# Float64 weights into float32 words by ACT and DVE, w_in without identity products, and a new issue order

## The chip, the cores and the metric

One Trainium2 chip, one of its cores. The metric is the device time of one launch in microseconds (us), the median of several runs. PE is the matmul engine, ACT the scalar engine, DVE the vector engine, POOL the general one; SP issues nearly all transfers (DMAs).

## The reference

Inputs: q, k, v of 8 batches x 8 heads x 576 rows x 64, and p of 8 x 8 x 32 x 64, all float32; w_in (512 x 1024), conv_w (3 x 1024) and w_out (1024 x 512) come out of NumPy as float64.

```python
packed = softmax(p @ k.T / 8) @ v                # 32 packed rows a head
attn   = softmax(q @ packed.T / 8) @ packed      # 576 rows a head
x      = attn with the heads side by side        # 8 x 576 x 512
h      = relu(x @ w_in)                          # 8 x 576 x 1024
conv   = sum over t of conv_w[t] * h shifted by t - 1 along the 576 rows
out    = (h * sigmoid(conv)) @ w_out             # 8 x 576 x 512, float32
```

## The kernel before

**Stages.** The 64 heads are taken as 16 groups g of four heads, two groups a batch b. Per group: k and q are loaded and transposed (`load_kq`, `head_transpose`: by PE with an identity for the first four groups, by DVE blocks after that), p is scaled and transposed (`queries`), and `attention(g)` does both softmaxes: PE makes scores, DVE the maxima `nm` and the sums, ACT the exponentials, and DVE leaves the second softmax transposed, as two float32r parts `a2hi` and `a2lo`. Per batch `packed_weight(b, hf)` multiplies the packed rows into w_in (L581), once for each half hf of its 1024 columns, and splits the product into `ghi` and `glo`; `ffn1(b, j)` multiplies that with a2 (L633), one of eight column blocks j at a time, and ACT and DVE do relu, convolution, gate and product into `hgt`. `ffn2(m)` takes 128 rows of the output at a time, 36 tiles m: ACT and DVE split `hgt` into `xhi` (L679) and `xlo` (L682), PE does 24 products with `wo_hi` and `wo_lo` (L698, tiles `fo` and `sm`), ACT copies the result to `o` (L703), SP sends it.

**Weights.** A weight comes as eight pieces i of 128 x 1024 float64, pieces 0 to 3 w_in, 4 to 7 w_out; each half of w_in's columns is two pieces, so `packed_weight(b, 1)` needs piece 3. SP loads a piece (`load_weight`, L296) as pairs of 32-bit words, 1024 KB, into one of three buffers (`stage`, and two in the unused `hgt[1]`). A float64's upper word holds sign, exponent and the first mantissa bits, its lower word the rest. `f64_parts` lets ACT read the upper words as float32 with a Prelu (L267: its scale undoes the exponent's other bias, its alpha does so for negative numbers), DVE shift (L269) and mask (L271) that into the leading part `t`, and DVE multiply the lower words by its power of two (L273) into the rest. Then PE adds the two parts in PSUM: `ident` times `t` and `minus` times the negative rest (L325), and ACT copies the sum out (L329): for w_in to `w_in_sb`; for w_out PE also subtracts `wo_hi`, the leading part rounded to float32r by ACT (L318), and the copy is `wo_lo`. conv_w goes the same way in small, with a DVE addition (L340) in place of PE.

**Order.** Every stage is a generator whose pieces are queued on an engine one at a time, and the table `ORDER` (two characters a piece) says which generator goes on next. An engine works in exactly that order; semaphores hold a piece until what it reads is there. The class `Flow` plays the table with estimated durations while the kernel is built and fills foreseen gaps of PE with `idle` products (L243), until the first `ffn2` tile has been issued; it decides nothing else.

Of the kernel before, what the change touches and what calls it, by code (L numbers as in the profile page):

```python
# [18 lines left out]


ORDER = (
    "3l3k3k3k3k3k3k3m000303033k3k0404040b0802040b3q0g0b0505010j06060c0c0c0j060j060c3u0o0r060e090e07070k053r3r3r3r0k06"
    "0e0k060k050f0e06060e3v0m0f0m0m06060s0s3v0a063v0e0e0m0m0s0r0r3s0d063v060s0606060n060d3r3w3t3t0n3t0d0d0u0e0e0u3r0u"
    "3n0h0i400p0q3t3v3x3v0e3t06063t0l0l0e3x0e3x0e0e0m0m46463y0l0l0w0m0u463x3x0e060e0e0v0e41410v4141460z0m0u0m0m0u420t"
    "3x41410e0u0e0z0m0m3z0e3z0m0m3z480t0z0t0u410m480u0t3z484717473z0m100u0u0m4849494747124a0u480u494912434848434a4944"
    "173z4312120u4a4a0u3z49174a130u494b434c454a4a154b4b4b131f124c434c4d4g1f0m0m4b4b4g4d454c0m434c4d4c4g0u4b0u4c4d434g"
    "4e4e1f4f0u0u4e14454d4d1k0x1c4h4h0u454d4f4e12124h4f4f124i45454e4f4h180y1n4e4e4i4f4f124i1a4i1a451n4j4k6e6e1a1a4i4j"
    "1a4i4j1g1b4i4k4k4j114k164j4k6f4j6f4k1n1b6e6e6e6e6e6e4l6e6e6e4l4j4k1i12121i6g4l1i1a1a1o194l6e1e1d6f6f4m4m1j4m1i1i"
    "4m4l4m126g121a1a4l4l1j6f6f6f4n6f6f4n124m1i1i1q1q1q1a1a6f4m1a126f6h3o6h1v1a4o4o4o4o4p4p4n4n1r1v1q1a6g6g6g6g6g201l"
    "6f6g6g6g1v4p6g4q4r23236h12121a124n4p4p1a4n12124o4o1q1t1s1w4o1r1a4n234p4p6i6h6h6h6h6h6h6h6h4q6h1a126i1y1q1q1y1y1a"  # L30
    "1a4q1m1a6i6i6i6i1i1y6i241h28216g6j4r4r1i1y6j4s4s4s4s1z4s1z4s6i6i6i6k6i1i1y261y4t1i261i4u4s4t4t4u262b1p6k1i4t4t4v"
    "4v6i1u1q6j6j4v1q4v272c4v6j26262b2b4u4t4u6j6j6j6j6j4v4v4u6j6j1q6l50271q1q1x1q502e504u1i1i4w4w4w4u1q1q4w4t1i2e2e4w"
    "3p4w6l1i294w1i6k6k6k2f2f6k6k6k6k6k2g4x6k2k4y2j1i1q4x4y6m4y4x4y6m6l1y1y226l4y6l4z4z2o6k1i4z4z1q4x6l6l6l6l6l4y6l1q"
    "1i4z26511y5126511q4y1q4x4x1q2e6m266m6m6m6m6m1y4x1y264z4z52532j2e6n536m6m251y6n2j525252526m2m2m53525352532e265426"
    "2m6o53532r2n2s6n6n6n6n555a1y6n546n546n6m2e541y5655552654546o545556566n6n2m6p572r2r57261y1y55566l2w552z572a5a2m1y"
    "6p565655566o6o6o6o6o6o2z6o1y1y2n58582z6o6o575a572626262d596p6q6q1y6p2h6o6p6p6p6p6p2e6p57585959585858596p6p2e3726"
    "5b5b2u5826572q59592626592m2e2e266q6q6q6q6q6q6q6r6r6q6s2i5b2u2e6s2p5c5c2u5c5d2m5c5c2e5e5d6q6q2u2m6n5e5e5c2e5d302x"
    "6r6r6r6r6r6r6r2u2m5c5d5d5d5e5e2v5f6r5d5e5f2u5k5g2v2e2e2e5e2e6r6r345f5g5k2u2l5h6s5h5h2e5f5k5f6s5h5h5f5f6s6s37376s"
    "2u32322m2m2e5i6s6s6s3f6t5h6s5i5i3c5h2m2t6t2u2m2m5j5i2m5i6u325g5j6t6t2m2m6u5g2m6t3e386t5i6t6t6t6t3f5j6t6t5g2e2m2u"
    "5l325g5g5j2m2m6v6v325j5j6u6u6u6u6u6u6u5i6u6u5m5l3f366u5m5m332u2u332u5j5m5m6v5n5n5n3a3a325n3g5o6w5m5m3a5o5o5o5l32"  # L40
    "355o5o5n5n5o6v6v6v3b6v3a5n3b5p6v5p2u3a6v32326v5q5p5q5q5r5r6w2y5u5u315q3i6v3a325p5p6v5q3i5p3i326w5p6w323a6w6w6s6w"
    "6w3i6w5r5r5q6x6x2u2u6w2u6w2u3a5s32325q6y3j5r5r3j2u6y6x6x6x6x6x6x6x6x5s2u2u5s6x6x5s6z3d5t6y5s5s6y6y6w6y3a6y6y5t5u"
    "5t3i6y6y6y6y6z5r395s3i3i5v3a3232325t5t5t5t3270706z5v6z3i3i6z6z6z6z6z6z3232326z6z5v5w713a3h3a3a5w5w5w5w5w5w705x5x"
    "5y5y5y70707070707070715y5z3i70725y645z5x5x5x3i723a71717171715z7171715z5x5x7171605y5z5z5y5z737272727272727272603i"
    "733i61603i72727060603a3a3a3i3a7474616061603i3i3a3a613a613i643i6273737364636362737373737361626262653i3i6373636363"
    "616362627575657474747474747474666666666674746767676866667575757569766868676775757575676765696969767569696a697568"
    "686a6a77776a7676767676767676686a6a686a6b786b6b6b6c7673766c6c6d6b6b6b6c6d6d786d6d777777777777777777776c6c6c6d6d79"
    "797878787878787878787a7a79797979797979797b7b7979787a7a7a7a7a7a7a7a7a7a7c7c7b7b7b7b7b7b7b7b7b7b7d7c7c7c7c7c7c7c7c"
    "7c7c7d7d7d7d7d7d7d7d7d7d7d"
)  # L50


# [133 lines left out]
def tile_packed_attention_conv_gate(  # L186
# [68 lines left out]
    def small(tag="sm"):  # L255
        return ps.tile([128, 512], F32, name=tag, tag=tag)

    def f64_parts(tiles, raw, m, after=(), take=(), sets=None):
# [8 lines left out]
        nc.scalar.activation(out=e, in_=up.bitcast(F32), func=AF.Prelu, scale=F64_REBIAS, alpha=-(2.0**32))  # L267
# [1 line left out]
        nc.vector.tensor_scalar(out=ti, in0=ei, scalar1=3, scalar2=None, op0=ALU.logical_shift_left)  # L269
# [3 lines left out]
        nc.vector.scalar_tensor_tensor(  # L273
            out=rest,
            in0=low,
            scalar=2.0**-52 if rest.dtype == F32 else -(2.0**-52),
            in1=e,
            op0=ALU.mult,
            op1=ALU.mult,
        )  # L280
# [17 lines left out]
    def weight(i):  # L298

        c, cols, src, st = weight_tile(i)  # L300
        hi, lo = (w[:, 2 * (i % 4) : 2 * (i % 4) + 2, :].rearrange("r c f -> r (c f)") for w in (wo_hi, wo_lo))
        token, tags = ("gw", ("ghi", "glo")) if i < 2 else ("x", ("xhi", "xlo"))
        parts = []

        def tiles():
            t, e = (wk.tile([128, DFF], F32, name="tmp", tag=tag) for tag in tags)
            parts.extend([(ident, t), (minus, lo)])
            return t, e, lo

        after = [("wd", i), "minus"] + ([("ws", i - 4)] if i >= 4 else [])  # L310
        if src.dtype != F32:
            yield from f64_parts(tiles, st, DFF, after, [token], [("wp", i)])
        else:
            yield Step("DVE", 0, after=after, take=[token])
            parts.append((ident, st))
        if i >= 4:
            yield Step("ACT", 905)
            nc.scalar.copy(out=hi, in_=parts[0][1])  # L318
            parts.append((minus, hi))
        ns = 2 * (864 + 234 * (len(parts) - 1))  # L320
        yield Step("PE", ns, take=["big"], give=[token], sets=[("ws", i)], cols=2 * (1536 + 512 * len(parts)))
        s = big()
        for hf in range(2):
            for k, (w, x) in enumerate(parts):
                nc.tensor.matmul(  # L325
                    out=s[:, hf, :], lhsT=w, rhs=x[:, 512 * hf : 512 * hf + 512], start=k == 0, stop=k == len(parts) - 1
                )
# [1 line left out]
        nc.scalar.copy(out=w_in_sb[:, c : c + 2, cols] if i < 4 else lo.rearrange("r (c f) -> r c f", c=2), in_=s)  # L329

    def conv_weight():
        src = conv_w.rearrange("k (j c) -> (k j) c", c=128)
        yield Step("POOL", 68, take=["s2", "s2"])
        st = [wk.tile([128, S], F32, name="s2", tag="s2") for _ in range(2)]
        if conv_w.dtype != F32:
            nc.gpsimd.dma_start(out=st[0][: 3 * NJ, :256].bitcast(I32), in_=src.bitcast(I32))
            t, e = st[1][: 3 * NJ, :128], st[1][: 3 * NJ, 128:256]
            yield from f64_parts(lambda: (t, e, e), st[0][: 3 * NJ, :256], 128)
            yield Step("DVE", 202)
            nc.vector.tensor_tensor(out=cw_raw, in0=t, in1=e, op=ALU.add)  # L340
# [420 lines left out]
```

## Time and profile before

| | |
|---|---|
| time, median of 3 runs | 421.45 us (421.42 to 421.62) |
| profiled execution, first to last instruction (its span) | 418.1 us; the trace holds no more of this execution's own time than that |
| median less span: what lies around it | 3.4 us |
| busy of the span: PE, DVE, ACT | 409.7, 342.4, 282.6 us |
| read from memory, written to it | 37.25 MB, 9.44 MB |

Busy time of PE includes the idle products. A share over the whole span mixes stages here: DVE and ACT have slack over the whole, and none in some of it, so the stages are read one by one. In the trace an instruction's time overlaps with the next one's start by some 0.07 us on DVE and 0.1 to 0.2 us on ACT, so the distance from one start to the next is what an instruction costs on a full engine.

### The profile page before, as it was taken

To read this page: it belongs to the slowest core of one execution; us is meant where nothing else is said; L and a number is where in the kernel's file an instruction comes from. 1 tells how busy PE (TensorE), PEld (TensorE's weight loads), DVE (VectorE), ACT (ScalarE), POOL (GpSimd) and SP (SyncE) were. 2 spreads that over 40 slices of the span, in tenths; PEclk is the share of its full clock that TensorE was granted. 3 is DMA by queue.
4 is the path that set the end of the run, shared out by engine and by line. 5 is a ranking of instruction groups with operands and counts; after the bars stand their busy time and mean duration, and the time that the engine had idled before them with its cause. 6 is when DMAs were issued, how large, how long until landed. Compare 5 with 4: busy or idle time off the path is not lost.

```text
span 418.1 us, 8176 instructions
## 1 busy us (share of the span) xinstructions
PE 409.7 (98%) x3355; PEld 325.4 (78%) x3355; DVE 342.4 (82%) x488; ACT 282.6 (68%) x480; POOL 1.6 (0%) x13
## 2 busy tenths in 40 slices
...
GB/s 300 362 374 302 242 172 104 56 83 171 200 52 176 89 180 110 2 141 80 28 164 141 138 59 123 98 53 2 133 26 2 25 52 19 57 27 25 52 50 50
DMA packets 135620, 47.21 MB, mean 113 GB/s; under 512 B 119700, under 2 KB 127892, under 8 KB 135584
## 3 DMA queue, kind: packets, MB, share of 16 engines
...
HBM read 37.25 MB, written 9.44 MB: 112 GB/s over the span
## 4 chain that ended last, share of the span: by engine, by line
PE 96%; ACT 2%; DMA 1%; issue 0%; POOL 0%; POOLq 0%; ACTq 0%
PE fo L698 45%; PE big L633 24%; PE big L325 5%; PE big L444 4%; PE sm L698 4%; PE big L581 3%; PE sm L507 3%; PE big L498 2%; PE big L428 2%; PE idle L243 2%; DMA s<-in_moe_conv_w_dram 1%; PE sm L471 1%; PE sm L523 0%; PE big L597 0%; ACT o L703 0%; ACT hbuf L645 0%
## 5 line engine op out<-in xcount | busy, mean ns | idle before, releaser
L698 PE MATMUL fo<-wo_hi,xhi 128*128 128x512 f32 x264 | 106.9, 405 | 0.7 <-ACT o L703 0.7
L698 PE MATMUL fo<-wo_lo,xhi 128*128 128x512 f32 x264 | 104.3, 395 | 0.0
L698 PE MATMUL fo<-wo_hi,xlo 128*128 128x512 f32 x264 | 104.3, 395 | 0.0
L651 DVE SCALAR_TENSOR_TENSOR hgt<-hbuf,cw,hgt 128x576 f32<-128x576 f32 x64 | 51.5, 808 | 13.9 <-ACT hgt L649 13.7
L698 PEld LDWEIGHTS fo<-wo_hi,xhi 128*128 128x128 f32 x264 | 49.6, 188 | 15.6 <-ACT o L703 2.4
L659 ACT ACTIVATE hgt<-hgt 128x576 f32<-128x576 f32 x64 | 43.6, 687 | 26.0 <-DVE hgt L655 25.7
L682 DVE TENSOR_TENSOR xlo<-hgt,xhi 128x1024 fp32r<-128x1024 f32 (+1 forms) x40 | 44.0, 1106 | 19.5 <-ACT xhi L679 19.2
L698 PEld LDWEIGHTS fo<-wo_hi,xlo 128*128 128x128 f32 x264 | 49.6, 188 | 11.7
L698 PEld LDWEIGHTS fo<-wo_lo,xhi 128*128 128x128 f32 x264 | 49.8, 188 | 9.3
L633 PE MATMUL big<-a2hi,ghi 128*128 128x288 f32 x256 | 56.2, 301 | 0.2 <-ACT glo L601 0.2
L661 DVE SCALAR_TENSOR_TENSOR hgt<-hgt,hbuf 128x576 f32<-128x576 f32 x64 | 47.0, 743 | 9.6 <-ACT hgt L659 9.3
L633 PE MATMUL big<-a2hi,glo 128*128 128x288 f32 x256 | 54.9, 295 | 0.0
L633 PE MATMUL big<-a2lo,ghi 128*128 128x288 f32 x256 | 54.7, 295 | 0.0
L655 DVE SCALAR_TENSOR_TENSOR hgt<-hbuf,cw,hgt 128x576 f32<-128x576 f32 x64 | 51.4, 811 | 0.9
L649 ACT ACTIVATE hgt<-hbuf,cw 128x576 f32<-128x576 f32 x64 | 49.8, 780 | 1.1
L645 ACT ACTIVATE hbuf<-big 128x576 f32<-128x576 f32 x64 | 41.7, 654 | 13.1 <-PE big L633 12.4
L703 ACT COPY o<-fo 128x512 f32<-128x512 f32 x33 | 19.3, 583 | 43.6 <-PE fo L698 37.2
L633 PEld LDWEIGHTS big<-a2hi,ghi 128*128 128x128 f32 x256 | 42.5, 189 | 6.9 <-DVE s L531 0.9
L679 ACT CAST xhi<-hgt 128x1024 fp32r<-128x1024 f32 (+1 forms) x40 | 38.3, 961 | 11.2 <-DVE hgt L661 4.7
L633 PEld LDWEIGHTS big<-a2lo,ghi 128*128 128x128 f32 x256 | 41.0, 188 | 0.0
L633 PEld LDWEIGHTS big<-a2hi,glo 128*128 128x128 f32 x256 | 41.0, 188 | 0.0
L487 DVE TENSOR_REDUCE nm<-big 128x1 f32<-128x576 f32 x16 | 12.0, 751 | 9.3 <-PE big L444 9.2
...
## 6 DMA issues: line engine op xcount, KB each, us to landing
...
v<-in_v_dram SPq DMA_DIRECT2D x16, 512.0 KB, 5.2
k<-in_k_dram SPq DMA_DIRECT2D x48, 144.0 KB, 4.7
q<-in_q_dram SPq DMA_DIRECT2D x48, 144.0 KB, 4.0
hgt<-in_moe_w_in_dram SPq DMA_DIRECT2D x3, 1024.0 KB, 8.6
hgt<-in_moe_w_out_dram SPq DMA_DIRECT2D x3, 1024.0 KB, 6.6
hgt<-in_k_dram SPq DMA_DIRECT2D x2, 576.0 KB, 3.9
hgt<-in_q_dram SPq DMA_DIRECT2D x2, 576.0 KB, 8.9
```

The lines of the kernel that those rows point to most:

```text
L325: nc.tensor.matmul(out=s[:, hf, :], lhsT=w, rhs=x[:, 512 * hf : 512 * hf + 512], start=k == 0, stop=k == len(parts) - 1)
L633: nc.tensor.matmul(out=t[:, hf, :SH], lhsT=w[:, gg, js], rhs=x[:, hf * SH : (hf + 1) * SH], start=n == 0, stop=n == 3 * NG - 1,)
L645: nc.scalar.activation(out=h[:, 1 : S + 1].rearrange("c (f s) -> c f s", f=2), in_=t[:, :, :SH], func=AF.Relu, scale=0.5)
L649: nc.scalar.activation(out=d, in_=h[:, 1 : S + 1], func=AF.Copy, scale=cw[:, NJ + j : NJ + j + 1])
L651: nc.vector.scalar_tensor_tensor(out=d, in0=h[:, 0:S], scalar=cw[:, j : j + 1], in1=d, op0=ALU.mult, op1=ALU.add)
L655: nc.vector.scalar_tensor_tensor(out=d, in0=h[:, 2 : S + 2], scalar=cw[:, 2 * NJ + j : 2 * NJ + j + 1], in1=d, op0=ALU.mult, op1=ALU.add)
L659: nc.scalar.activation(out=d, in_=d, func=AF.Tanh)
L661: nc.vector.scalar_tensor_tensor(out=d, in0=d, scalar=1.0, in1=h[:, 1 : S + 1], op0=ALU.add, op1=ALU.mult)
L679: nc.scalar.copy(out=hi[:, :, o], in_=src)
L682: nc.vector.tensor_tensor(out=lo[:, :, o], in0=src, in1=hi[:, :, o].bitcast(F32), op=ALU.subtract)
L698: nc.tensor.matmul(out=t, lhsT=x[:, c, :], rhs=w[:, c, :], start=c + i == 0, stop=c == NJ - 1 and i == 2)
L703: nc.scalar.copy(out=o, in_=t)
```

## The change

`f64_parts` becomes `narrow`, which makes whole float32 words without PE. ACT's Prelu stays, but writes in place over the upper words. DVE scales the lower words by 2^-29 and limits them to 7, in place, as integers (L265): these are the three mantissa bits that are missing. One last DVE instruction shifts the upper word left by three and ors the bits in (L270). For w_in its output is `w_in_sb` itself, and PE and ACT have nothing more to do. For w_out the whole word goes through PE once (`ident` times the word, `minus` times `wo_hi`: four products a piece, six before). conv_w loses its addition and one of its two buffers. `ORDER` is a new table.

```diff
 ORDER = (
-    "3l3k3k3k3k3k3k3m000303033k3k0404040b0802040b3q0g0b0505010j06060c0c0c0j060j060c3u0o0r060e090e07070k053r3r3r3r0k06"
...
+    "00043m03030404033q02080b0b04063r0c06050b0j0601070605050c0c06073k3r3k060c0g063r0e053k06063l3u060e0e0a0k3k063v0k0f"
...
-    def f64_parts(tiles, raw, m, after=(), take=(), sets=None):
+    def narrow(out, raw, m, after=(), take=(), sets=None):
         pair = raw.rearrange("r (c t) -> r c t", t=2)
-        up = pair[:, :, 1].bitcast(I32)
-        low = pair[:, :, 0].bitcast(U32)
-        yield Step("ACT", 93 + m * 14 // 15, after=after, take=take)
-        t, e, rest = tiles()
-        ti, ei = t.bitcast(I32), e.bitcast(I32)
-        nc.scalar.activation(out=e, in_=up.bitcast(F32), func=AF.Prelu, scale=F64_REBIAS, alpha=-(2.0**32))
+        up = pair[:, :, 1]
+        low = pair[:, :, 0]
+        yield Step("ACT", 93 + m * 14 // 15, after=after)
+        nc.scalar.activation(out=up, in_=up, func=AF.Prelu, scale=F64_REBIAS, alpha=-(2.0**32))
         yield Step("DVE", 68 + m * 100 // 192)
-        nc.vector.tensor_scalar(out=ti, in0=ei, scalar1=3, scalar2=None, op0=ALU.logical_shift_left)
-        yield Step("DVE", 68 + m * 100 // 192)
-        nc.vector.tensor_scalar(out=ei, in0=ti, scalar1=-0x800000, scalar2=None, op0=ALU.bitwise_and)
-        yield Step("DVE", 69 + m * 100 // 96, sets=sets)
+        nc.vector.tensor_scalar(
+            out=low.bitcast(I32), in0=low.bitcast(U32), scalar1=2.0**-29, scalar2=7.0, op0=ALU.mult, op1=ALU.min
+        )
+        yield Step("DVE", 69 + m * 100 // 96, take=take, sets=sets)
+        out = out()
         nc.vector.scalar_tensor_tensor(
-            out=rest,
-            in0=low,
-            scalar=2.0**-52 if rest.dtype == F32 else -(2.0**-52),
-            in1=e,
-            op0=ALU.mult,
-            op1=ALU.mult,
+            out=out,
+            in0=up.bitcast(I32),
+            scalar=3,
+            in1=low.bitcast(I32),
+            op0=ALU.logical_shift_left,
+            op1=ALU.bitwise_or,
         )
...
     def weight(i):
...
+        after = [("wd", i)]
+        if i < 4:
+            dst = w_in_sb[:, c : c + 2, cols]
+            if src.dtype != F32:
+                yield from narrow(lambda: dst.bitcast(I32), st, DFF, after, sets=[("wp", i), ("w", i)])
...
+            return
...
-            for k, (w, x) in enumerate(parts):
+            for k, (w, x) in enumerate(((ident, wide[0]), (minus, hi))):
...
-        nc.scalar.copy(out=w_in_sb[:, c : c + 2, cols] if i < 4 else lo.rearrange("r (c f) -> r c f", c=2), in_=s)
+        nc.scalar.copy(out=lo.rearrange("r (c f) -> r c f", c=2), in_=s)
```

What the table does to the engines' queues is seen at three places. In these rows `hgt_77` and `stage` are the buffers of the weight pieces, `hgt_76` holds k and q of the first two groups, `v`, `k`, `q` are later groups' loads, `tmp` is `t` or `e` before and the whole word of a w_out piece after. The changed kernel's line numbers are a few lower: its L293, L263, L591 are L296, L267, L593 before.

SP's queue near its start, before (the pieces of w_in are loaded in the order 0, 2, 1, 3; the row with x2 is 1 and 3):

```order
L394 DMA hgt_76<-in_q_dram 128x1152
L296 DMA hgt_77<-in_moe_w_in_dram 128x2x1024
L394 DMA k<-in_k_dram 128x1152
L378 DMA v<-in_v_dram 128x4x256
L382 DMA v<-in_v_dram 64x4x64
L296 DMA stage<-in_moe_w_in_dram 128x2x1024
L394 DMA k<-in_k_dram 128x1152
L378 DMA v<-in_v_dram 128x4x256
L382 DMA v<-in_v_dram 64x4x64
L394 DMA hgt_76<-in_q_dram 128x1152
L296 DMA hgt_77<-in_moe_w_in_dram 128x2x1024 x2
```

And after, from piece 2 on:

```order
L293 DMA stage<-in_moe_w_in_dram 128x2x1024
L392 DMA hgt_76<-in_q_dram 128x1152
L293 DMA hgt_77<-in_moe_w_in_dram 128x2x1024
L376 DMA v<-in_v_dram 128x4x256
L380 DMA v<-in_v_dram 64x4x64
L392 DMA k<-in_k_dram 128x1152
L293 DMA stage<-in_moe_w_out_dram 128x2x1024
L392 DMA q<-in_q_dram 128x1152
L376 DMA v<-in_v_dram 128x4x256
L380 DMA v<-in_v_dram 64x4x64
L293 DMA hgt_77<-in_moe_w_in_dram 128x2x1024
L293 DMA hgt_77<-in_moe_w_out_dram 128x2x1024
```

Piece 3 of w_in now stands behind the first w_out piece and a third group's q and v; ahead of piece 2 the same loads stand as before, with k and p at the head exchanged and w_in's piece 0 third.

ACT's queue before, from the Prelu of piece 3 on:

```order
L267 ACTIVATE tmp<-hgt_77 128x1024
L329 COPY w_in_sb<-big 128x2x512
L559 CAST a2hi<-a2t 128x576
L329 COPY w_in_sb<-big 128x2x512
L434 COPY qT<-big 128x640
L541 ACTIVATE s_493<-s_493 128x576
L518 ACTIVATE pb<-sm,rs 128x128
L593 CAST ghi<-big 128x1024
L434 COPY qT<-big 128x512
L267 ACTIVATE tmp<-stage 128x1024
L601 CAST glo<-big 128x1024
```

And after, around the Prelu of piece 3, which is the `L263` row ahead of `wo_hi`:

```order
L591 CAST ghi_468<-big_426 128x1024
L489 ACTIVATE a1_483,sm1_484<-big_446,nm_481 128x576
L432 COPY qT_459<-big_460 128x640
L599 CAST glo_469<-big_426 128x1024
L516 ACTIVATE pb_524<-sm_492,rs_418 128x128
L432 COPY qT_459<-big_519 128x512
L524 COPY ppT_534<-sm_532 128x128
L557 CAST a2hi_538<-a2t_527 128x576
L263 ACTIVATE hgt1_77<-hgt1_77 128x1024
L321 CAST wo_hi_74<-tmp_544 128x1024
L499 COPY a1T_582<-big_561 128x640
L263 ACTIVATE hgt1_77<-hgt1_77 128x1024
```

The copies to `w_in_sb` are gone, and the first packed weight (`ghi`, `glo`) and a second `a2hi` now come ahead of piece 3.

DVE's queue before, from piece 0 on:

```order
L269 TENSOR_SCALAR tmp<-tmp 128x1024
L271 TENSOR_SCALAR tmp<-tmp 128x1024
L273 SCALAR_TENSOR_TENSOR wo_lo<-hgt_77,tmp 128x1024
L567 TENSOR_SCALAR rs<-sm_275 128x1
L569 RECIPROCAL rs<-rs 128x1
L487 TENSOR_REDUCE nm<-big 128x1
L531 STREAM_TRANSPOSE s_327<-big 128x576
```

And after, from piece 0 to the second group's `nm` and beyond:

```order
L265 TENSOR_SCALAR hgt_77<-hgt_77 128x1024
L270 SCALAR_TENSOR_TENSOR w_in_sb<-hgt_77 128x2x512
L265 TENSOR_SCALAR s_199<-s_199 24x128
L485 TENSOR_REDUCE nm<-big 128x1
L270 SCALAR_TENSOR_TENSOR cw_raw<-s_199 24x128
L529 STREAM_TRANSPOSE s_273<-big 128x576
```

Piece 0 and conv_w now stand around the second group's maximum (`nm`), where piece 0 came behind it before and conv_w ahead of everything.

More of the change, by code (lines that the diff above doesn't have):

```diff
@@ L27 @@
[L27 to L41, printed above, removed]
@@ new lines @@
+    "0l410e463w463y060u0u0e0l410e0n0m0e0v0e460v0l0m0l0e0m0m0q0e0p413x410m0e0u480u3z49480m3x480m0t4a3x3z490m0t0m47490u"
+    "4a470u0u47484a3z48490u0m3n480t0t0u49490z4a483z4a470u490z0w0z4b4a10424b44174b4c120u4a0m15450u4b4c0u124d4b4c434c45"
+    "12170m174c3z4d0m0x4g3z4c430m4b1f12414g0u134c144g120m0u4b1f4g454d4e4e4f1f41434d0u4e0m121c18431t4f450u13124h4e3o0y"
+    "0u4h434d454f4h4f4e430u4d0u4h124e451a4d4f4i4e4f4i1a124f4j1g1n4k6e1a6e1a1n4j1b4j4i1a6e4k1k114j4i4j6f1b4i6e4j6f6e4j"
+    "6e6e1n6e4k1e1i1a124i1i126e6e161i4i1a4l1a6e4l121v4m1a4l4k126f1o6f3p4k4l1d4m1v121j1i1v6f4m121u4k6g1i6f194l6f1q4k1q"
@@ new lines @@
+    "645x71713a5x5y71715y3a715z713i5y3i3i646x5y72603a723i3i5x715z603i5z713i3a5z61605z60726072726172723i723a5z71626064"
+    "737262706072726261737263743a3i62623i7374616273653i61627363617373637363737373666361746674746365676663747474676666"
+    "6867756668676674746975686774696875757575686969687565677568767569747569756776756a69736a6b776a766a7676766a6c6a776b"
+    "766a6c6c7676766d76776c6d6b6d7778776c6d776b776c78777777776d6b78776b787878766b78786d6c6d787879797979787a7979797979"
+    "79797a7b7a7a7a7a7a7a7a7a7b7b7b7c797c7b7b7a7b7b7b7b7c7c7a7b7d7c7d7c787c7c7c7c7b7d7d7c7c7d7d7d7d7d7d7d7d"
@@ L300, in weight @@
         c, cols, src, st = weight_tile(i)
-        hi, lo = (w[:, 2 * (i % 4) : 2 * (i % 4) + 2, :].rearrange("r c f -> r (c f)") for w in (wo_hi, wo_lo))
[L302 to L310, printed above, removed]
+        after = [("wd", i)]
@@ new lines, in weight @@
+        if i < 4:
+            dst = w_in_sb[:, c : c + 2, cols]
+            if src.dtype != F32:
+                yield from narrow(lambda: dst.bitcast(I32), st, DFF, after, sets=[("wp", i), ("w", i)])
+            else:
+                yield Step("DVE", 1135, after=after, sets=[("wp", i), ("w", i)])
+                nc.vector.tensor_copy(out=dst, in_=st.rearrange("r (c f) -> r c f", c=2))
+            return
+        hi, lo = (w[:, 2 * (i % 4) : 2 * (i % 4) + 2, :].rearrange("r c f -> r (c f)") for w in (wo_hi, wo_lo))
@@ L311, in weight, with whole @@
+        wide = []
+        def whole():
+            wide.append(wk.tile([128, DFF], F32, name="tmp", tag="xhi"))
+            return wide[0].bitcast(I32)
         if src.dtype != F32:
-            yield from f64_parts(tiles, st, DFF, after, [token], [("wp", i)])
+            yield from narrow(whole, st, DFF, after, ["x"], [("wp", i)])
         else:
[L314 to L319, printed above, removed]
@@ L320, in weight @@
-        ns = 2 * (864 + 234 * (len(parts) - 1))
-        yield Step("PE", ns, take=["big"], give=[token], sets=[("ws", i)], cols=2 * (1536 + 512 * len(parts)))
+            yield Step("DVE", 1135, after=after, take=["x"], sets=[("wp", i)])
+            whole()
+            nc.vector.tensor_copy(out=wide[0], in_=st)
+        yield Step("ACT", 905, after=["minus"])
+        nc.scalar.copy(out=hi, in_=wide[0])
+        yield Step("PE", 2 * (864 + 234), take=["big"], give=["x"], cols=2 * 2560)
         s = big()
```

43 lines of the change are left out of this document (22 added, 21 removed).

## The prediction

> **What bounds the kernel now.** I read the page first, then busy time by stage, then the chain of work that ended last.
>
> ```profile
> span 418.1 us, 8176 instructions
> PE 409.7 (98%) x3355; PEld 325.4 (78%) x3355; DVE 342.4 (82%) x488; ACT 282.6 (68%) x480; POOL 1.6 (0%) x13
> ```
> ```profile
> 20.00:40.00 20.00, 20.00 (x236) 11.48 (x228) 19.50 (x35) 18.53 (x33) 0.00 (x0) 1.00 1.06 361
> 60.00:80.00 20.00, 20.00 (x185) 14.59 (x184) 19.28 (x28) 19.50 (x34) 0.00 (x0) 1.00 0.51 74
> 84.00:414.00 330.00, 329.32 (x2555) 267.58 (x2553) 274.35 (x379) 209.01 (x350) 0.00 (x0) 1.00 0.42 82
> ```
>
> The second set is busy time by stretch: length, then PE, weight loads, DVE, ACT, POOL, then PE's granted clock, the DMA engines' share and GB/s. There are two regimes. From 84 us on PE works 329.3 of 330 us, and DVE and ACT have slack. Between 20 and 80 us PE, DVE and ACT are all full, and until 40 us the DMA engines too. The chain (start, us, what) shows what PE does at the edges:
>
> ```profile
> 24.49 2.20 PE big L325 x6
> 42.05 2.67 PE big L325 x8
> 76.89 2.66 PE big L325 x8
> 84.23 4.20 PE fo L698 x18
> 414.55 0.58 ACT o L703
> ```
>
> The identity products (L325, from the first w_in piece at 24.5 us to the last w_out piece at 76.9) are all done before the first `fo` product at 84.2 us. Counted in the two instruction orders, PE's work from the first `fo` to the end is the same, and so is what stands ahead of it, except L325 (40 products before, 16 after) and the idle ones (33 before, 42 after). So the time is: start of the first `fo`, plus 330.3 us of the same work (84.2 to 414.5), plus what follows it. **The change is worth what it moves the first `fo`**, less any stall that it makes later.
>
> **The change, part by part.**
>
> PE. A w_in piece took 2.2 us, four of them 8.8; a w_out piece goes from 2.67 to about the 2.2 of four products, four times 0.47 is 1.9. Together 10.7 us. The nine idle products more cost up to 3.0:
>
> ```profile
> L243 PE MATMUL idle<-ident 128*128 128x128 f32 x66 | 11.0, 314 | 2.5 <-POOL ident masks.py:199 2.5
> ```
>
> (66 records are 33 products, 0.33 us each.) If PE were the bound, the first `fo` would come 7.7 us earlier, and 10.7 if the idle products only fill gaps. It was full, but with 11 us of idle products, which stand where something else was late.
>
> ACT. It does the same Prelus to the weights and loses the four copies to `w_in_sb`. On its path to the first `xhi`, which `fo` needs:
>
> ```profile
> 20.32 1.21 ACT L267 ACTIVATE tmp<-stage 128x1024 f32<-128x1024 f32 x1
> 30.14 1.16 ACT L267 ACTIVATE tmp<-hgt 128x1024 f32<-128x1024 f32 x1
> 79.31 0.84 ACT L649 ACTIVATE hgt<-hbuf,cw 128x576 f32<-128x576 f32 x1
> 79.99 1.07 ACT L329 CAST wo_lo<-big 128x1024 fp32r<-128x1024 f32 x1
> 80.88 1.12 ACT L679 CAST xhi<-hgt 128x1024 fp32r<-128x1024 f32 x1
> ```
> ```profile
> 20.32:80.88 60.56, 60.08 (x603) 41.16 (x588) 59.42 (x93) 58.30 (x97) 0.00 (x0) 1.00 0.89 212
> 30.14:80.88 50.74, 50.26 (x493) 35.05 (x493) 49.69 (x77) 49.40 (x81) 0.00 (x0) 1.00 0.86 180
> ```
> ```profile
> L329 ACT COPY w_in_sb<-big 128x1024 f32<-128x1024 f32 x4 | 4.1, 1021 | 0.5 <-PE big L325 0.5
> L593 ACT CAST ghi<-big 128x1024 fp32r<-128x1024 f32 x16 | 16.2, 1014 | 1.7 <-PE big L581 1.6
> L601 ACT CAST glo<-big 128x1024 fp32r<-128x1024 f32 x4 | 4.1, 1027 | 0.0
> L559 ACT CAST a2hi<-a2t 128x576 fp32r<-128x576 f32 x16 | 10.8, 673 | 6.4 <-DVE a2t L555 6.4
> L434 ACT COPY kT<-big 128x640 f32<-128x640 f32 x4 | 2.8, 708 | 1.6 <-PE big L428 1.6
> L501 ACT COPY a1T<-big 128x640 f32<-128x640 f32 x16 | 11.1, 691 | 3.5 <-PE big L498 3.5
> ```
>
> The next instruction starts 0.10 to 0.18 us before one ends (79.99 and 1.07 long, the next at 80.88), so I take the rows' times less that. From the Prelu of piece 2, the second that is loaded (20.32), to `xhi` (80.88) ACT idled 2.3 of 60.56 us. In the new order four copies (0.90 each: 3.6) and one L649 (0.7) leave that stretch, and six small pieces join it that stood ahead of that Prelu: two evictions to `kT` (0.6 and, at 512 columns, 0.5), one to `a1T` (0.6), and one each to `pT`, `pm` and `cw`, of 128 columns or fewer (an estimate of 0.4 for the three): 2.1. So 60.56 - 3.6 - 0.7 + 2.1 = 58.4.
>
> When can that Prelu start? When piece 2 has landed, which is its issue plus the time to landing. The rows: issues of pieces 0 and 2; their times to landing and the sizes of a v and a k load (q's are like k's); issue and landing of piece 3.
>
> ```profile
> 2.72 0.53 SPq L296 DMA_DIRECT2D hgt<-in_moe_w_in_dram  x1
> 5.23 0.61 SPq L296 DMA_DIRECT2D stage<-in_moe_w_in_dram  x1
> ```
> ```profile
> hgt<-in_moe_w_in_dram SPq DMA_DIRECT2D x1, 1024.0 KB, 8.6
> stage<-in_moe_w_in_dram SPq DMA_DIRECT2D x1, 1024.0 KB, 12.0
> v<-in_v_dram SPq DMA_DIRECT2D x16, 512.0 KB, 5.2
> k<-in_k_dram SPq DMA_DIRECT2D x2, 576.0 KB, 11.1
> ```
> ```profile
> L296 SPq DMA_DIRECT2D hgt<-in_moe_w_in_dram x1: 368/368/368, 20.0 to 20.0; - x1
> DMA to landing us min/median/max: 8.5/8.5/8.5
> ```
>
> Piece 0 landed at 11.3, piece 2 at 17.2, piece 3 at 28.5 us. The same loads stand ahead of piece 2 after the change, so it lands at 17.2 again, and its Prelu can run 3.1 us sooner than at 20.32: `xhi` at 17.2 + 58.4 = 75.6 against 80.88, 5.3 us earlier.
>
> The second test is piece 3, which its column half waits for; its Prelu stood at 30.14. From piece 2 to it came k, v and q of 1664 KB and two pieces (1 and 3), 3712 KB in 11.3 us, 328 KB a us. Now a w_out piece, a q and a v come in between, 5824 KB, 17.7 us: piece 3 lands at 34.9. From its Prelu to `xhi` ACT took 50.74 us; in the new order 9.5 us less stand there, by the same rows: three copies 2.7, a Prelu 1.0, `ghi` and `glo` 1.8, two `a2hi` 1.1, L649 0.7, two evictions to `qT` (`kT`'s size) 1.1, and an exponential over 576 columns and two small ones 1.1. That is 41.2, `xhi` at 76.1, 4.8 earlier. I take the middle of the two, **5.0 us**.
>
> DVE. Two bit passes and a multiply a piece become one integer pass and a shift-or.
>
> ```profile
> 55.01 0.69 DVE L269 TENSOR_SCALAR tmp<-tmp 128x1024 int32<-128x1024 int32 x1
> 55.62 0.81 DVE L655 SCALAR_TENSOR_TENSOR hgt<-hbuf,cw,hgt 128x576 f32<-128x576 f32 x1
> 59.87 1.22 DVE L273 SCALAR_TENSOR_TENSOR wo_lo<-hgt,tmp 128x1024 fp32r<-128x1024 uint32 x1
> 61.01 0.76 DVE L661 SCALAR_TENSOR_TENSOR hgt<-hgt,hbuf 128x576 f32<-128x576 f32 x1
> ```
>
> Start to start, L269 costs 0.61 and L273 1.14. No row shows L265, which reads and writes every second word. Its neighbours are L269 (same size, one tensor in, adjacent words) and L273 (same size, two in, one of them every second word). L269 is the same instruction, so I take 0.61 and keep 1.14 as the other end. L270 has both inputs at every second word; L273 with one such costs 1.14, which I take. The Prelus already read every second word at 1.05; writing so I take as free, and above that no row bounds it.
>
> The Trainium skill ("VectorE: DVE Perf Modes", Mode 2×_2P) asks, for two elements a cycle in float32, for one source, both ends in SBUF and even outer sizes, and names no unit step; by that rule L265 stays at 0.61 and the sum as it is. The same page says of its Mode 1× that "fp32, weird strides, PSUM operands — all work", which would be 1.14 and the second rival below. No run here shows which.
>
> DVE's own path went from the second group's `nm` to `xlo` without a gap worth naming:
>
> ```profile
> 16.14 0.76 DVE L487 TENSOR_REDUCE nm<-big 128x1 f32<-128x576 f32 x1 [3.95 <-PE big L444]
> 82.03 1.23 DVE L682 TENSOR_TENSOR xlo<-hgt,xhi 128x1024 fp32r<-128x1024 f32 x1
> ```
>
> That is 65.9 us. Sixteen passes leave (9.8) and seven L265 come (4.3); one multiply (1.1), one L651 (0.7) and two tiny ones (0.3) leave; one `kT` transpose of 1152 columns (1.3) and conv_w's L270 (0.2) come: 59.8. If that `nm` came no sooner, DVE would be at `xlo` at 75.9; the v that it now waits for follows piece 0's set and lands near 12.8 (512 KB at the 358 KB a us that came between pieces 0 and 2), which would give 72.6. ACT lets it start after `xhi`, at 76.6 to 77.2. So DVE is not the bound, with little to spare.
>
> Queues. conv_w goes behind two groups' work; only `ffn1` needs its `cw`, so it costs nothing, and ACT and PE no longer stand behind its load. SP moves piece 3 back, counted above, and with it what is behind: the fifth group's k, which DVE transposes.
>
> ```profile
> 47.63 1.32 DVE L417 STREAM_TRANSPOSE kT<-k 128x1152 f32<-128x1152 f32 x1
> k<-in_k_dram SPq DMA_DIRECT2D x48, 144.0 KB, 4.7
> ```
>
> After the change a w_out piece, q, v and p, some 2240 KB, are between piece 3 and that k: 34.9 + 6.8 + 4.7 = 46.4. DVE comes to the transpose 14 instructions behind piece 3's L270, near 48: 1 to 2 us to spare, so I put nothing in the sum and a share of the second rival's chance here.
>
> Sum: first `fo` 5.0 us earlier, PE behind it unchanged: 418.1 - 5.0 = 413.1 us of span, and with the 3.4 us around it 416.5; against the median of 421.45 itself, 5.0 less is 416.4, which I give.
>
> **The rivals.**
>
> - *PE was the bound.* For it: its row reads 20.00 of 20. Against it: 11 us of idle products, and ACT's 58.3 of 60.56. Then 7.7 to 10.7 us come: 410.7 to 413.7.
> - *L265 at one word a cycle.* 0.53 more on seven pieces is 3.7 us: DVE reaches `xlo` at 76.3 to 79.6, 2.4 to 5.7 earlier than before, and as ACT and DVE wait for each other many times over I put it at 417.5 to 420.3. The same range holds if 1 to 4 us of new waits come with the new order.
> - *Piece 3 comes too late, and the kernel is slower.* At 34.9 the gain is 4.8, and each us later costs one: from a landing at 39.7 on (259 KB a us behind piece 2, for 328) it is slower, at 43 by 3.3 us, 424.8. For it: SP issues in order, and ahead of piece 3 now stands a w_out load that needs `stage` free. Against it: `stage` is free by about 20 us, 15 us ahead.
> - *Nothing moves*, since the first `fo` hangs on something that no row names: 421.5.
>
> **How the numbers follow.** ACT's chain as summed, 415.0 to 417.5: 0.53. PE was the bound: 0.15. L265 slow or new waits: 0.18. Nothing: 0.05. Piece 3 late: 0.09. About 0.2% (0.85 us) is what a measurement of this kernel can tell from no change. Faster is the first three, 0.86; same 0.05; slower 0.09. The range leaves out the slower case and half of the PE case, and reaches into the third: 412.4 to 419.4.
>
> **What the profile after would show.** The first `fo` product near 79 us and 330.3 us from it to PE's end. No L325 for w_in, 2.2 us for a w_out piece. ACT full from piece 2's Prelu near 17.2 to `xhi` near 76, with piece 3's Prelu near 35. L265 0.69 us long; 1.22 is the second rival. I am wrong if PE stalls behind the first `fo`, if piece 3 lands past 37, or if the in-place words cost ACT or DVE more than their neighbours' rows.

## The result and the profile after

| | median, us | runs | lowest to highest | granted clock of the runs |
|---|---|---|---|---|
| before | 421.49 | 4 | 421.42 to 421.62 | 0.998 to 1.000 (in 54 more runs beside the experiments, 420.19 to 422.32 us) |
| after | 415.98 | 4 | 414.90 to 417.86 | 0.991 to 1.000 |

The ratio is 0.9871, 95% interval 0.9845 to 0.9897: 1.3% or 5.5 us faster, 0.4 us from the forecast. The profiled execution after took 415.89 us with a span of 414.1, so 1.8 us lie around it. Each run lists its mean granted TensorE clock, and after the change the longer runs have the lower clock; more on that below.

The page, the stretches and the chain of waits after, in the columns in which they were shown of before:

```profile
span 414.1 us, 8121 instructions
PE 401.9 (97%) x3341; PEld 321.9 (78%) x3341; DVE 335.6 (81%) x478; ACT 278.3 (67%) x476; POOL 1.6 (0%) x13
...
```
```profile
20.00:40.00 20.00, 19.54 (x264) 14.39 (x264) 19.67 (x36) 19.45 (x36) 0.00 (x0) 1.00 1.01 350
60.00:80.00 20.00, 20.00 (x170) 14.57 (x169) 19.14 (x30) 19.97 (x33) 0.00 (x0) 1.00 0.79 135
80.00:410.00 330.00, 328.47 (x2555) 267.44 (x2554) 273.45 (x379) 209.17 (x351) 0.00 (x0) 1.00 0.36 79
```
```profile
2.70 10.44 DMA hgt<-in_k_dram
27.50 11.40 DMA hgt<-in_moe_w_out_dram
45.82 7.80 DMA hgt<-in_moe_w_out_dram
60.24 2.23 PE big L326 x6
68.01 4.55 PE big L326 x12
80.29 4.20 PE fo L696 x18
404.89 5.62 PE sm L696 x24
```

The first `fo` stands at 80.29, before at 84.23, and PE ends at 404.89 + 5.62 = 410.51: 330.2 us behind it, as before (330.3). In these two executions all of the gain lies ahead of the first `fo`. What is new on the chain are transfers: the second group's k (issued at 2.70) and two w_out pieces. ACT's Prelus of pieces 2, 3 and 6 and its first `xhi`, and the rows of the new DVE instructions (mean ns in the second number):

```profile
19.61 1.16 ACT L263 ACTIVATE stage<-stage 128x1024 f32<-128x1024 f32 x1
36.05 1.21 ACT L263 ACTIVATE hgt<-hgt 128x1024 f32<-128x1024 f32 x1
53.65 1.13 ACT L263 ACTIVATE hgt<-hgt 128x1024 f32<-128x1024 f32 x1 [1.39 <-DMA hgt<-in_moe_w_out_dram]
77.39 1.05 ACT L677 CAST xhi<-hgt 128x1024 fp32r<-128x1024 f32 x1
```
```profile
L265 DVE TENSOR_SCALAR hgt<-hgt 128x1024 int32<-128x1024 uint32 x6 | 4.1, 675 | 0.0
L270 DVE SCALAR_TENSOR_TENSOR w_in_sb<-hgt 128x1024 int32<-128x1024 int32 x3 | 3.7, 1222 | 0.0
L263 ACT ACTIVATE hgt<-hgt 128x1024 f32<-128x1024 f32 x6 | 7.0, 1162 | 3.4 <-DMA hgt<-in_moe_w_in_dram 1.8 <-DMA hgt<-in_moe_w_out_dram 1.4
```

L265 takes 0.68 us for 1024 columns of every second word: the duration of its neighbour L269 (0.69), not of L273 (1.22); L270 takes L273's 1.22. Of the two rules that the prediction weighed, that of Mode 2×_2P ("VectorE: DVE Perf Modes" in the Trainium skill) agrees with this row.

### The profile page after: what moved, and what is told of

It is laid out like the page before. It is cut to its first block, busy times and chain, and to the rows that moved or that the text cites. A ratio compares the mean times of both kernels' runs of the same rounds, so it can differ in the third digit from the quotient of the medians.

```text
span 414.1 us, 8121 instructions
## 1 busy us (share of the span) xinstructions
PE 401.9 (97%) x3341; PEld 321.9 (78%) x3341; DVE 335.6 (81%) x478; ACT 278.3 (67%) x476; POOL 1.6 (0%) x13
## 4 chain that ended last, share of the span: by engine, by line
PE 86%; DMA 7%; ACT 3%; DVE 2%; issue 1%; SPq 0%; ACTq 0%
PE fo L696 45%; PE big L631 22%; DMA hgt<-in_moe_w_out_dram 5%; PE sm L696 4%; PE big L442 4%; PE big L579 3%; DMA hgt<-in_k_dram 3%; PE sm L505 2%; PE big L496 2%; PE big L326 2%; ACT hbuf L643 1%; PE big L426 1%; DVE w_in_sb L270 1%; ACT hgt L647 1%; DVE s L529 0%
## 5 line engine op out<-in xcount | busy, mean ns | idle before, releaser
L696 PE MATMUL fo<-wo_hi,xhi 128*128 128x512 f32 x264 | 108.1, 410 | 0.7 <-ACT o L701 0.7
```

Of the source, the lines that this page charges most:

```text
L696: nc.tensor.matmul(out=t, lhsT=x[:, c, :], rhs=w[:, c, :], start=c + i == 0, stop=c == NJ - 1 and i == 2)
```

## The experiments

The theories: **mine**, that landings and then ACT's chain set the first `fo`, and PE's saved products mostly turn into waits; that **PE was the bound**; that **DVE** had no slack; and that either **the conversion or the order** alone brought it all. All kernels ran beside the kernel before, 4 to 12 runs each, in four jobs. Of the twelve results only e_again and e_dve_back fell where the theory that I call mine had put them, e_act_back 0.2 us outside; the others are told one by one.

| label | median, us | ratio to before, 95% | granted clock |
|---|---|---|---|
| e_old_order | 420.24 | 0.9974 (0.9960 to 0.9988) | 0.987 to 0.996 |
| e_old_order_filled | 419.00 | 0.9951 (0.9935 to 0.9966) | 0.999 to 1.000 |
| e_pe_back | 423.98 | 1.0067 (1.0044 to 1.0090) | 0.992 to 1.000 |
| e_act_back | 417.77 | 0.9921 (0.9896 to 0.9946) | 0.992 to 1.000 |
| e_dve_back | 418.74 | 0.9937 (0.9920 to 0.9955) | 0.995 to 1.000 |
| e_again | 415.11 | 0.9872 (0.9841 to 0.9903) | 0.992 to 1.000 |
| e_no_idle | 414.91 | 0.9851 (0.9835 to 0.9866) | 0.999 to 1.000 |
| e_k1_first | 418.64 | 0.9948 (0.9929 to 0.9967) | 0.990 to 0.996 |
| e_p3_first | 418.52 | 0.9931 (0.9907 to 0.9955) | 0.978 to 0.996 |
| e_loads | 416.11 | 0.9878 (0.9861 to 0.9896) | 0.982 to 0.995 |
| e_loads_3first | 417.06 | 0.9920 (0.9891 to 0.9949) | 0.975 to 0.996 |
| e_loads_idle | 416.08 | 0.9873 (0.9855 to 0.9891) | 0.998 to 1.000 |

**Conversion and order.** The old table, less the characters of the pieces that are gone:

```diff
+IDLE = {(3, 2): 5, (4, 3): 2, (12, 3): 4, (6, 4): 6, (14, 6): 1, (156, 1): 10, (161, 3): 2, (38, 8): 1, (128, 5): 1, (145, 5): 1}
 ORDER = (
-    "00043m03030404033q02080b0b04063r0c06050b0j0601070605050c0c06073k3r3k060c0g063r0e053k06063l3u060e0e0a0k3k063v0k0f"
+    "3l3k3k3k3k3k3m000303033k3k0404040b0802040b3q0g0b0505010j06060c0c0c0j060j060c3u0o0r060e090e07070k053r3r3r0k060e0k06"
...
-                if self.busy not in self.done:
-                    self.fill(at)
+                if (n, order[: k + 1].count(n)) in IDLE:
+                    self.warm(IDLE[n, order[: k + 1].count(n)])
```

`IDLE` says ahead of which PE piece of which generator how many idle products stand: the 33 of before, at their places.

> The new conversion under the old issue order: the old table with only the pieces left out that the conversion no longer has, and the 33 idle products of before at their old places. If the first fo product is set by landings and ACT's chain (mine), the four copies to w_in_sb that ACT loses are worth up to 4 x 0.90 = 3.6 us, less what turns into waits: 417.9 to 419.5, first fo at 80.6 to 82.5. If PE was the bound, the 10.7 us of products that leave come in full: 410.7 to 413. If the gain needs the new table (order alone): 421 to 422, first fo still near 84.

It brought 1.1 us, less than I had expected, and no run had the full clock. Stretch 30 to 40 us of before, of this run, and of the next one (PE's busy time is the second number, its granted clock the third from the right):

```profile
30.00:40.00 10.00, 10.00 (x119) 5.25 (x117) 9.70 (x18) 9.45 (x17) 0.00 (x0) 1.00 1.07 350
```
```profile
30.00:40.00 10.00, 6.84 (x89) 3.77 (x89) 9.44 (x16) 6.23 (x10) 0.00 (x0) 0.66 1.06 360
```
```profile
30.00:40.00 10.00, 10.00 (x153) 7.97 (x155) 8.44 (x16) 7.22 (x13) 0.00 (x0) 1.00 1.07 351
```

PE, full in this stretch before, now idles 3.2 of 10 us, 2.8 of them for a load of q, and its clock falls to 0.66. The next run fills such places: the old table, with `self.fill(at)` left as it was, which puts in 73 idle products.

> The new conversion under the old issue order, as in the run before, but with the gaps that the lost products leave filled: 73 idle products in place of 33, where the estimated durations foresee a gap. If the conversion alone is worth ACT's four copies, 3.6 us, and holes with a lower clock ate most of it there (mine): clock 1.000 and 417 to 418.5. If the conversion alone is worth about 1 us: 420 to 420.5 again; if idle products take time on the path: 421 or more.

The clock is back at 1.00 and 1.2 more us come: the conversion alone is worth 2.45 us (421.45 - 419.00, one job), less than ACT's 3.6, and the new table on top of it the other 3.9 (419.00 to 415.11 for e_again in the same job). In the old order the copies' time stayed partly empty: in e_old_order_filled ACT was busy 54.56 of the 59.34 us from piece 2's Prelu to `xhi`,

```profile
20.31:79.65 59.34, 58.74 (x652) 44.74 (x637) 55.96 (x86) 54.56 (x94) 0.00 (x0) 1.00 0.85 216
```
```profile
19.61:77.39 57.78, 55.91 (x609) 39.87 (x608) 55.29 (x89) 55.80 (x99) 0.00 (x0) 1.00 0.91 243
36.05:77.39 41.34, 39.93 (x385) 28.67 (x370) 39.18 (x59) 39.77 (x66) 0.00 (x0) 1.00 0.87 201
```

and 55.80 of 57.78 in the changed kernel (second fence, with the stretch from piece 3's Prelu below it). So the conversion alone is not the gain. The new table with the old conversion was not run, so what the order alone would bring is not shown.

**Each engine's saved work given back**, into the changed kernel:

```diff
 # e_pe_back: in weight(), for each of the four w_in pieces
+                extra = ps.tile([128, 512], F32, name="extra", tag="fo")
+                for _ in range(10):
+                    nc.tensor.matmul(out=extra[:, :128], lhsT=ident, rhs=ident, start=True, stop=True)
 # e_act_back: at the same place
+                nc.scalar.copy(
+                    out=wo_lo[:, 6:8, :].rearrange("r c f -> r (c f)").rearrange("r (c f) -> r c f", f=128),
+                    in_=ident.unsqueeze(1).broadcast_to([128, 8, 128]),
+                )
 # e_dve_back: in narrow(), behind L265
+        if m == DFF:
+            nc.vector.tensor_scalar(
+                out=low.bitcast(I32), in0=low.bitcast(U32), scalar1=1.0, scalar2=7.0, op0=ALU.mult, op1=ALU.min
+            )
```

> The changed kernel with PE's saved products given back: behind each of the four w_in pieces PE gets ten more products of the idle kind (128 columns), about 0.22 to 0.33 us each, 8.8 to 13 us in all; nothing reads them. If PE does not set the first fo (mine): up to 2.5 us, 416 to 418.5. If PE is the bound: all of it, 424.8 or more.

> The changed kernel with ACT's four lost copies given back: behind each w_in piece ACT copies 1024 columns of constants to a part of wo_lo that is overwritten later, about 0.9 us each, 3.6 in all; nothing waits for them. If ACT's chain from the Prelu of the second loaded piece on sets the first fo (mine): three of the four stand behind that Prelu, so 2.7 us, 418 to 419.5. If PE or DVE sets it: 0 to 1 us, 416 to 417.

> The changed kernel with a second pass of DVE over the low words of all eight pieces (an integer pass of the same size that changes nothing), 0.61 us each, 4.9 in all: about what L265 at one word a cycle would have cost (4.3). By my prediction DVE has some slack and ACT and DVE wait for each other, so 1 to 3 us: 417 to 419. If DVE is the bound in the front: 4.9, 420.9. If it has slack enough: under 0.8, below 416.8.

Since the runs differ in clock, I compare those at 0.998 or more. The changed kernel has six (two jobs): mean 414.9, 414.18 to 415.89. PE's 9.7 us more gave 422.87 (one run): 8.0, most of it, and three times what I had expected; at 0.996 it is 7.5 (four runs of mean 423.89 against two of 416.38). ACT's four copies of 1.04 us, some 3.7 from start to start, gave 416.86 (three runs): 2.0 where I had 2.7. DVE's eight passes, 4.9 by the 0.61 of the prediction, gave 418.17 (three runs): 3.3, just above the 1 to 3 that I had. So none of the three has slack enough to swallow its part; each passes on between half and four fifths. That speaks for one chain through all three engines, not for ACT's alone, and PE passes on most; by itself e_pe_back comes close to what PE as the bound would give. The first ten products of e_pe_back, the scores behind them, and the `nm` that waits for the scores:

```profile
18.24 2.50 PE L305 MATMUL extra<-ident 128*128 128x128 f32 x20
20.67 0.72 PE L445 MATMUL big<-kT,pT 64*32 64x288 f32 x16
```
```profile
21.49 0.76 DVE L488 TENSOR_REDUCE nm<-big 128x1 f32<-128x576 f32 x1 [7.12 <-PE big L445]
```
```profile
18.02 0.76 DVE L485 TENSOR_REDUCE nm<-big 128x1 f32<-128x576 f32 x1 [3.36 <-PE big L442]
```

The last row is the changed kernel's. The lump stands ahead of the second group's scores, and all that follows on DVE and ACT comes later. Of the 3.5 us between the two `nm` some 2.5 are the lump; the rest had come before it, behind a stretch of lower clock that this execution has and that is shown below.

**PE's amount of work, and the clock.** Two runs: the changed kernel again for its spread, and without any idle product:

```diff
     def warm(n):
-        t = ps.tile([128, 512], F32, name="idle", tag="fo")
+        return
```

> The changed kernel once more, unaltered, for the spread of its times and the granted clock of each run. If what makes a run longer is a stretch of lower clock behind the wait of PE for k near 10.5 to 13.2 us (mine), the times follow the clock: about 415 to 416 at 1.000, about 1.2 us more for each 0.004 less. If the spread has another cause, runs of one clock differ by as much as the whole.

> The changed kernel without its 42 idle products (14.5 us of PE's busy time). If they only fill time in which PE waits, and the clock does not hang on them: 416, within 0.8. If they take PE's time on the path: faster, down to 410. If the clock falls behind holes in PE's work (mine, since the runs of the other kernels that were longer had a lower granted clock): clock 0.98 to 0.995 in every run and 417.5 to 421.

The spread: over both jobs, six runs at 0.998 to 1.000 took 414.18 to 415.89, two at 0.996 took 416.06 and 416.70, and two at 0.991 and 0.992 took 417.86 and 418.95. The steps are as I had them; at the full clock 1.7 us of spread remain. No long run of the changed kernel itself was profiled. Where the lower clock comes from is seen in two profiled executions, of the changed kernel (clock 1.000) and of e_pe_back (0.996), whose programs are alike up to 18 us. From 6.83 us on in steps of 3.41 (the steps are mine; PE's busy time second, its granted clock third from the right):

```profile
6.83:10.24 3.41, 3.41 (x36) 2.76 (x35) 0.76 (x1) 1.15 (x4) 0.00 (x0) 1.00 0.98 385
10.24:13.65 3.41, 0.75 (x7) 0.56 (x6) 1.25 (x4) 2.06 (x6) 0.00 (x0) 1.00 1.08 347
13.65:17.07 3.42, 3.42 (x58) 2.76 (x56) 1.02 (x2) 2.54 (x5) 0.00 (x0) 1.00 1.02 393
```
```profile
6.83:10.24 3.41, 3.27 (x36) 2.25 (x34) 0.76 (x1) 1.41 (x4) 0.00 (x0) 1.00 0.98 386
10.24:13.65 3.41, 0.78 (x6) 0.79 (x7) 1.53 (x4) 1.77 (x6) 0.00 (x0) 0.96 1.07 351
13.65:17.07 3.42, 3.42 (x19) 3.42 (x18) 0.73 (x2) 2.01 (x4) 0.00 (x0) 0.54 1.03 385
```

PE waits for the second group's k there, and its ten transposes of k and q come next, in the changed kernel, in e_pe_back, and (third) in e_no_idle:

```profile
13.18 1.31 PE L426 MATMUL big<-ident,hgt 128*128 128x128 f32 x10 [2.66 <-DMA hgt<-in_k_dram]
```
```profile
12.87 1.95 PE L429 MATMUL big<-ident,hgt 128*128 128x128 f32 x10 [2.67 <-DMA hgt<-in_k_dram]
```
```profile
12.23 2.37 PE L426 MATMUL big<-ident,hgt 128*128 128x128 f32 x10 [3.46 <-DMA hgt<-in_k_dram]
```

A wait of 2.66 us left the clock at 1.00, one of 2.67 was followed by 0.54: the new order has put a hole into PE's work behind which the clock falls in some runs. One stretch of 3.4 us at 0.54 lowers the mean over some 418 us by 0.004, which is the step between the runs (1.000, 0.996, 0.992). That the changed kernel's own longer runs fell at this hole is argued from there. The kernel before, whose PE worked 9.98 of the 10 us from 10 to 20, never fell below 0.998.

But e_no_idle refutes what I made of it. Without the 14.5 us of idle products the time is 414.91 against 415.11 in the same job, no difference that these runs can tell, and all four runs are at 0.999 or 1.000, 414.16 to 415.31. So the idle products take no time on the path, in their places; and in these four runs the clock did not need them. Without them PE works at half pace until about 17 us (the ten transposes take 2.37 us for 1.31). What is late by that, piece 2's Prelu at 19.93 for 19.61, is made up by piece 3's (36.15 for 36.05).

Together with e_pe_back: the 42 idle products, where no one waited for PE, cost nothing; 40 products of the same kind behind the w_in pieces, the first ten ahead of scores, cost 8 us. PE's amount of work was not the bound; where in the chain it stands decides.

**The landings.** Can the start come earlier? First, piece 0 behind the second group's k on SP, and its conversion and piece 2's later on ACT and DVE:

```diff
 # SP's queue from its second entry on
+L392 DMA hgt_76<-in_k_dram 128x1152
-L293 DMA hgt_77<-in_moe_w_in_dram 128x2x1024
 L392 DMA hgt_76<-in_q_dram 128x1152
-L392 DMA hgt_76<-in_k_dram 128x1152
 L376 DMA v<-in_v_dram 128x4x256
 L380 DMA v<-in_v_dram 64x4x64
+L293 DMA hgt_77<-in_moe_w_in_dram 128x2x1024
```

> The changed kernel with piece 0 of w_in loaded behind the second group's k and the first v instead of ahead of them, with the places of pieces 0 and 2 on ACT and DVE moved back accordingly, so that ACT has other work while piece 2 is still on its way; the six idle products ahead of that k's transposes are left out. If the landings set the start of ACT's full stretch (mine): PE's wait of 2.66 us for that k goes, the clock stays at 1.000, and up to 2.5 us come: 412.5 to 415, unless piece 3's landing near 35.8 holds ACT, then 414.5 to 415.5 with an idle ACT ahead of its Prelu. If ACT's chain from piece 2 on is fixed as summed: 415 to 416.

It is 3.5 us slower than e_again in the same job. The wait for k is gone, and a longer one for the second group's q has come, with a lower clock behind it:

```profile
20.85 0.74 PE L426 MATMUL big<-ident,hgt 128*128 128x128 f32 x5 [3.19 <-DMA hgt<-in_q_dram]
```
```profile
17.07:20.48 3.41, 0.59 (x6) 0.35 (x4) 2.31 (x4) 1.49 (x4) 0.00 (x0) 1.00 1.02 408
20.48:23.89 3.41, 3.04 (x30) 2.26 (x30) 0.63 (x1) 1.83 (x3) 0.00 (x0) 0.74 1.07 334
```

Second, without idle products, piece 3 ahead of piece 5 on SP alone:

```diff
+L293 DMA hgt_77<-in_moe_w_in_dram 128x2x1024
 L293 DMA stage<-in_moe_w_out_dram 128x2x1024
 L392 DMA q<-in_q_dram 128x1152
 L376 DMA v<-in_v_dram 128x4x256
 L380 DMA v<-in_v_dram 64x4x64
-L293 DMA hgt_77<-in_moe_w_in_dram 128x2x1024
```

> The kernel without idle products, with one load moved: piece 3 of w_in ahead of the first w_out piece (piece 5), so that piece 3 lands about 6 us sooner and piece 5 up to 3 us later; the engines' queues are unchanged. If piece 3's landing near 35.8 us does not bind because ACT is full from piece 2's Prelu on (my sum, in which both conditions came out nearly equal): 414 to 415.5, no change; or up to 1.5 us slower where ACT then waits for piece 5 near 30 us. If piece 3's landing binds: 412.5 to 414.

Not faster: it is 3.6 us slower than e_no_idle (414.91, in another job), and slower than either side of my expectation; ACT now waits for piece 5, and the clock is low in every run:

```profile
32.25 1.11 ACT L263 ACTIVATE stage<-stage 128x1024 f32<-128x1024 f32 x1 [1.22 <-DMA stage<-in_moe_w_out_dram]
```

So this run does not settle whether piece 3's landing held the changed kernel. The changed kernel's own trace does, for its execution: the Prelu of piece 3 (36.05, above) starts without a wait.

Third, all early loads in the order of need (k, p, k, q, v, piece 0, k, q, piece 2, v, piece 1, the rest as it was), conversions moved back accordingly: without idle products, then with piece 3 ahead of piece 5 on all queues, then the first with 42 idle products at the places of its waits (`IDLE` as in e_old_order).

> The kernel without idle products, with the first loads in the order in which the groups need them: k of the second group, q and v of the first, piece 0, then the second group's q ahead of piece 2 and its v ahead of piece 1; pieces 0, 2 and 1 are converted a few instructions later on ACT and DVE. This closes the wait for k (3.46 us) and the two that took its place when only piece 0 was moved. If the front is a chain through landings and all three engines (mine): about 1.5 us at piece 1's Prelu, of which the next landings (piece 5, piece 3) may take some back: 413 to 414.5. If the waits only move again: 415 to 418.

> The run before with piece 3 loaded and converted ahead of piece 5 as well, so that no engine waits for piece 5's buffer near 30 us. If the landings of pieces 5 and 3 take the gain of the new load order back (mine): 412 to 413.5. If the front's end is set by ACT's amount of work alone: as the run before.

> The kernel with the first loads in the order of need, now with 42 idle products again, placed where PE waited in the run without them (ahead of the loads of k and q of groups 2 and 3 above all). If holes of PE behind a warm stretch lower the granted clock, and that cost this order its gain (mine): clock at 0.996 to 1.000 and 412.5 to 414.5. If the clock is not what held it: 415.5 to 417, as without them. If idle products take PE's time on the chain: 417 or more.

None is faster than the changed kernel, and none came near what I expected; with piece 3 ahead it is 0.95 us slower still (417.06). e_loads has a low clock in all its runs; e_loads_idle has the full clock and the same time, 416.08 for 416.11, so against my expectation the full clock, with the idle products that came with it, brought nothing. That these products took back what the clock gave is not excluded, and the two ran in different jobs. The waits of e_loads_idle on transfers, PE's and then ACT's:

```profile
22.81 0.90 PE L505 MATMUL sm<-v,a1T 128*32 128x64 f32 x40 [1.15 <-DMA v<-in_v_dram]
26.82 0.74 PE L426 MATMUL big<-ident,k 128*128 128x128 f32 x5 [0.88 <-DMA k<-in_k_dram]
32.37 0.74 PE L426 MATMUL big<-ident,q 128*128 128x128 f32 x5 [1.54 <-DMA q<-in_q_dram]
```
```profile
30.68 1.12 ACT L263 ACTIVATE stage<-stage 128x1024 f32<-128x1024 f32 x1 [1.05 <-DMA stage<-in_moe_w_out_dram]
54.54 1.12 ACT L263 ACTIVATE hgt<-hgt 128x1024 f32<-128x1024 f32 x1 [1.72 <-DMA hgt<-in_moe_w_out_dram]
```

What is loaded sooner makes something else late: to 40 us the DMA engines are full (share 1.01 in the stretch from 20 to 40 of the changed kernel). That no order of the loads would help is not shown; three did not.

## Why the prediction was right, and where it was not

- **The frame held.** The 330.3 us behind the first `fo` came out at 330.2, and the gain is what the first `fo` moved: 3.9 us in the profiled execution, 5.4 in the profiled one of e_again (78.79), both at a clock of 1.000.
- **The order of loads was misread.** "The same loads stand ahead of piece 2 after the change, so it lands at 17.2 again, and its Prelu can run 3.1 us sooner". Piece 2 was issued at 5.85 for 5.23 and took 13.3 us for 12.0, to 19.15:

```profile
5.85 0.65 SPq L293 DMA_DIRECT2D stage<-in_moe_w_in_dram  x1
```
```profile
stage<-in_moe_w_in_dram SPq DMA_DIRECT2D x1, 1024.0 KB, 13.3
```
  But its Prelu, at 19.61, did not wait for it: it followed the second group's exponentials at once, and these came late, since ACT had stood idle until PE had that group's k. This k took 3.9 us to land before; now piece 0 and a q are issued ahead of it, and it took 10.4. The sum has no term for it. ACT's rows in the profiled execution, then PE's and ACT's in that of e_again:

```profile
14.53 0.69 ACT L432 COPY qT<-big 128x640 f32<-128x640 f32 x1 [2.23 <-PE big L426]
18.88 0.74 ACT L489 ACTIVATE a<-big,nm 128x576 f32<-128x576 f32 x1 [0.18 <-DVE nm L485]
```
```profile
12.33 1.31 PE L426 MATMUL big<-ident,hgt 128*128 128x128 f32 x10 [1.90 <-DMA hgt<-in_k_dram]
18.75 1.16 ACT L263 ACTIVATE stage<-stage 128x1024 f32<-128x1024 f32 x1
26.56 0.37 ACT L516 ACTIVATE pb<-sm,rs 128x128 f32<-128x128 f32 x1 [1.13 <-PE sm L505]
52.11 1.16 ACT L263 ACTIVATE hgt<-hgt 128x1024 f32<-128x1024 f32 x1
75.88 1.05 ACT L677 CAST xhi<-hgt 128x1024 fp32r<-128x1024 f32 x1
```
  In e_again PE has that k 0.85 us earlier (12.33 for 13.18), and the Prelu of piece 2 is 0.86 earlier. But this lead is gone by piece 3's Prelu (36.33 for 36.05): ACT has waited 1.13 us for products that need a v, PE 1.24 for that v itself. So the start of ACT's stretch, on which the first of the two sums rests, did not set its end in these executions.
- **The ACT chain fits in its lengths, in part by luck.** From piece 2's Prelu to `xhi` it took 57.8 us for 58.4, from piece 3's 41.3 for 41.2; piece 3's Prelu stood at 36.05 for 35. But the 41.3 hold a wait of 1.39 us for piece 6 that the sum does not name. In e_again that wait is missing: its piece 6 Prelu (52.11) and its `xhi` (75.88) both come 1.5 us earlier, though its piece 3 Prelu stands at 36.33. So `xhi` came 3.5 us earlier than before in the profiled execution, and in e_again the 5.0 that were summed, from a later start and a shorter chain; and 1.5 us of spread between two executions at the full clock is the landing of piece 6.
- **"The 3.4 us around it" was wrong**, and made up for that. It was a median less the span of one execution. With span and time of each run, 2.1 lie around the kernel before (mean of 54 runs) and 1.8 around the changed one. So the forecast's span of 413.1 was 1.0 too short and its surroundings 1.6 too long; two errors that nearly cancel, which is luck. With 2.1 around its 418.1 the profiled execution before took some 420.2 us (an estimate), some 1.2 less than the median; that, and the 0.3 less around it, is why the medians differ by 5.5 us and the two spans by 4.0.
- **"PE was the bound" fell**, by e_no_idle; but the ground that I gave against it, PE's 11 us of idle products, told only of amount. That the place of PE's work counts, so that 9.7 us more cost 8.0, I had not seen.
- **DVE** had the slack that I gave it and no more: the rival at one word a cycle was priced at 1.1 to 3.9 us above the forecast for 3.7 us of work, and 4.9 us cost 3.3.
- **The queues**: no engine waits for `cw` or for the fifth group's k, as forecast. The wait for piece 6 I had not named.
- **The range** has no term for the spread of the runs; before's three lay 0.2 us apart. The changed kernel's ten runs lie 4.8 us apart (414.18 to 418.95), 1.7 of that at the full clock; the kernel before, over 54 runs at 0.998 or more, 2.1.

The kernel with the lowest median is e_no_idle: 1.5% faster than before (0.9835 to 0.9866), level with the changed kernel at its full clock, and in its four runs without the long ones.
